# Changing the widths of the first three held-back x transposes from 2, 2, 2 chunks to 1, 2, 3

## The chip, the cores and the metric

The kernel runs on one core of one Trainium2 chip. The metric is the device time of one execution in microseconds. The kernel before takes 265.04 us (median of the first three runs, 264.27 to 265.58). A verdict of faster or slower needs a difference of over 2%. The question here is smaller than that by an order of magnitude, so much of this document is about telling a difference of 0.1% from noise, and about seeing in a trace what the clock on the wall cannot resolve.

Names used below: a *chunk* is 128 of the 2,048 rows of x. PE is TensorE's matmul stream and PEld its weight loads, DVE is VectorE, ACT ScalarE, POOL GpSimd, SP SyncE (and SPq its queue, which issues DMAs).

## The reference

```python
# x: [1, 2048, 640] bf16
g = sigmoid((x * gate_w).sum(-1, keepdims=True))
# branch A: linear attention
q, k, v = split(x @ wqkv)            # 32 heads of 20
pq, pk = phi(q), phi(k)              # phi(t) = (t + 1 if t > 0 else exp(t)) + 1e-6
o = (pq @ (pk^T v)) / (pq . sum(pk) + 1e-6)
a = o @ wo
# branch B: a mixer MLP with layer norms, w1, w2, w3, w4  (cut)
return g * a + (1 - g) * b
```

Only the first product of branch A matters here: `k = x @ wk`, which the kernel computes chunk by chunk as its first stage. The matmul contracts over the 640 features, so it needs x with features on the partitions: the transposed tile `xT`.

## The kernel before

At the start the kernel loads x chunks 0 and 1 and the five pieces of `wk` by plain DMAs. Chunks 0 and 1 are transposed on PE (`turn`); chunks 2 to 15 are transposed by the DMA engines on their way in (`load_xT`). Those transposes are *held back*: one column of chunk 2's place in `xT` is written by DVE after the first PE transposes, and the first DMA transpose, which writes over that column, has to wait for it. All later transposes stand behind it on the SP queue. So the k weights go first.

```python
    def load_xT(c0, c1):
        sp.dma_start_transpose(xT[:, :, c0 * P:c1 * P], x2[c0 * P:c1 * P, :])
    # ... (cut)
    load_x(0, 1)
    aq.dma_start(g5[:], gate_w.rearrange("(c p) -> c p", p=P))
    load_wk(sp, 1)
    load_wk(aq, 0)
    load_x(1, 2, aq)
    load_wk(sp, 3)
    load_wk(aq, 2)
    load_wk(sp, 4)

    def late_loads():
        for c0, c1 in ((2, 4), (4, 6), (6, 8), (8, 10), (10, 12), (12, 16)):
            load_xT(c0, c1)
        sp.dma_start(wq_sb, wqkv_v[:, :, 0:D])
        # ... (cut: the other x loads and weights)

    def k_mm(pt, c, dcs, first=0, last=DC - 1):
        for dc in dcs:
            for hf in range(2):
                n = HD + hf
                nc.tensor.matmul(pt[:, hf, 0:n], lhsT=xT[:, dc, c * P:(c + 1) * P],
                                 rhs=wk_sb[:, dc, hf * HD:hf * HD + n], start=(dc == first), stop=(dc == last))
    # ... (cut)
    def turn(c):                    # chunks 0 and 1: transpose on PE
        for pt, a, b in turns:
            # ... (cut: five PE transposes in two groups)
            # ... (cut: DVE copies the group into xT)
            if c == 0 and a == 0:
                nc.vector.tensor_copy(wk_sb[:, :, D], pt[:, 1, 0:DC])
                nc.vector.memset(xT[:, 0:1, 2 * P:2 * P + 1], 0.0)     # holds the transposes back

    turn(0)
    late_loads()
    # ... (cut)
    warmup(1, TS)
    for n, dc in enumerate(k0_order):          # chunk 0, in the order in which wk arrives
        if n == 3:
            turn(1)
        elif 1 <= n < 3:
            warmup(1, 2 * P)
        k_mm(kp, 0, (dc,), first=k0_order[0], last=k0_order[-1])
    k_evac(kp, 0)
    for c in range(1, NCH):                    # chunks 1 to 15
        pt = pair()
        k_mm(pt, c, range(DC))
        k_evac(pt, c)
    # then the q stage, which reads all of xT
```

Of the kernel before, what the change touches and what calls it, by code (L numbers as in the profile page):

```python
# [16 lines left out]
def kernel(  # L17
# [100 lines left out]
    def load_x(c0, c1, q=sp):  # L118
        q.dma_start(x_sb[:, c0:c1, 0:D], x2[c0 * P:c1 * P, :].rearrange("(c p) d -> p c d", p=P))

    def load_xT(c0, c1):
        sp.dma_start_transpose(xT[:, :, c0 * P:c1 * P], x2[c0 * P:c1 * P, :])
# [11 lines left out]
    load_wk(sp, 4)  # L134

    def late_loads():
        for c0, c1 in ((2, 4), (4, 6), (6, 8), (8, 10), (10, 12), (12, 16)):
            load_xT(c0, c1)
        sp.dma_start(wq_sb, wqkv_v[:, :, 0:D])
        load_x(2, 8)  # L140
        load_x(8, 16)
        sp.dma_start(wv_sb[:], wqkv_v[:, :, 2 * D:3 * D])
        sp.dma_start(w1_sb[:], B_w1.rearrange("(c p) f -> p c f", p=P))
        for g in range(NG):
            sp.dma_start(wo_sb[:, g, :], A_wo[row0[g]:row0[g] + P, :])
        for g in range(4):
            sp.dma_start(w2_sb[:, g, :], B_w2[CG * g:CG * g + P, :])
            sp.dma_start(w2_sb[32 * g:32 * (g + 1), 4, :], B_w2[CG * g + P:CG * (g + 1), :])
        sp.dma_start(w3_sb[:], B_w3.rearrange("(c p) f -> p c f", p=P))
# [73 lines left out]

    turn(0)
    late_loads()
    for dc in range(DC):
        for g in range(4):
# [399 lines left out]
```

## Time and profile before

| | before |
|---|---|
| time, first three runs | 265.04 us (264.27 to 265.58) |
| span of the profiled execution | 262.8 us |
| PE busy | 259.1 us |
| first transpose issued / landed | 4.26 / 8.50 us |
| chunk 2's k weight loads begin | 8.55 us |
| q stage's first weight load | 27.50 us |

From the page, the busy time of each engine (time, share of the span, instructions) and the granted clock in 40 slices:

```profile
PE 259.1 (99%) x1738; PEld 159.9 (61%) x1738; DVE 142.7 (54%) x283; ACT 82.7 (31%) x123; POOL 20.2 (8%) x65
...
PEclk9999999999999999999999999999999999999999
```

PE is busy in 99% of the span, so whatever stops it for a moment should be added to the time. The chain of work that ended last, cut to the first 60 us (columns: start, duration, what), shows one piece that is not PE, DVE or issue:

```profile
4.21 0.05 DVE xT L218
4.26 4.24 DMA xT<-in_A_x_dram
8.50 0.05 issue
8.55 19.25 PE pp L185 x140
27.80 21.58 PE pp L247 x100
```

The 140 k matmuls of chunks 2 to 15 run in one piece after the first transpose has landed. But the 4.24 us of that transfer are not lost: PE is working on chunks 0 and 1 meanwhile. What it costs is in the tables of waits of PE and PEld (who waited for what: total us, times, longest):

```profile
PE pp L185 <- DMA xT<-in_A_x_dram: 0.2, 1, 0.2
...
PEld L185 <- DMA xT<-in_A_x_dram: 0.5, 1, 0.5
```

The weight load's 0.5 us is the better measure of the delay, because matmul ends are modelled and the weight load is what has to read `xT`. The timeline of PEld from 8.2 us (start, duration, what, count, idle before and its releaser) shows it in place. A timeline keeps loads in one line as long as none of them comes after more than 0.15 us of idle time; after this line no k weight load waits again.

```profile
8.54 11.42 PEld L185 LDWEIGHTS <-xT 128*128 128x128 bf16 x85 [0.53 <-DMA xT<-in_A_x_dram]
```

The first two transposes on the SP queue, each from a timeline of a narrow window, and the time from issue to landing of five of the six (the view places no landing for the first, whose semaphore later transfers share; its own records give 4.24 us):

```profile
4.26 1.48 SPq L122 DMA_TRANSPOSE xT<-in_A_x_dram  x1
...
5.79 1.67 SPq L122 DMA_TRANSPOSE xT<-in_A_x_dram  x1
...
DMA to landing us min/median/max: 4.2/4.6/5.8
```

Where an exact landing or the start of a chunk is quoted below, it is read from the trace's individual records: a transfer has landed when the last of its 16 completion records is in, and chunk c starts with the (10c+1)th weight load of the k stage.

### The profile page before, as it was taken

Reading aid. Unit: us, or ns where it says so; the run is one execution under the profiler, and the core shown is the slowest. Engines: PE = TensorE matmul, PEld = TensorE weight load, DVE = VectorE, ACT = ScalarE, POOL = GpSimd, SP = SyncE. Lnnn points to the kernel's source line nnn. Section 1 sums busy time; section 2 is a strip of 40 time slices with the busy share of each in tenths; the row PEclk is TensorE's granted clock in tenths of the full one; section 3 lists DMA queues with packets and bytes.
Section 4 is the critical chain, followed back from the end, with each engine's and each line's share of the span. In section 5 each row is a group of like instructions: output and inputs, shape, how many; then the busy total and the mean of one; then the engine's idle time right before and its main releaser. Section 6 shows DMA issues by size and latency. Waiting matters only on the chain.

```text
span 262.8 us, 4268 instructions
## 1 busy us (share of the span) xinstructions
PE 259.1 (99%) x1738; PEld 159.9 (61%) x1738; DVE 142.7 (54%) x283; ACT 82.7 (31%) x123; POOL 20.2 (8%) x65
## 2 busy tenths in 40 slices
PE   8999999999999999999999999999999999999995
PEld 4677555788755644555577555567565577555553
DVE  2688778899947998955403464413456223112132
ACT  1555454321166236622502222412131332142200
POOL 5000040012220040001000001000001000000000
PEclk9999999999999999999999999999999999999999
DMA  6999987016672566700132000051100051100011
GB/s 200 193 203 379 364 229 299 0 27 125 125 98 58 107 122 163 241 0 2 25 75 77 25 0 2 0 100 52 50 0 4 0 100 52 50 0 2 0 50 50
DMA packets 45757, 23.98 MB, mean 91 GB/s; under 512 B 35114, under 2 KB 44970, under 8 KB 45738
## 3 DMA queue, kind: packets, MB, share of 16 engines
q1 hardware_dynamic: 45296, 23.22, 34.6%
q10 hardware_dynamic: 442, 0.49, 0.5%
q8 instruction: 13, 0.21, 0.4%
q14 instruction: 6, 0.05, 0.1%
HBM read 12.21 MB, written 2.62 MB: 56 GB/s over the span
## 4 chain that ended last, share of the span: by engine, by line
PE 97%; DMA 2%; DVE 0%; issue 0%
PE pp L504 22%; PE pp L471 21%; PE pp L319 8%; PE pp L455 8%; PE pp L424 8%; PE pp L353 8%; PE pp L247 8%; PE pp L185 7%; DMA xT<-in_A_x_dram 2%; PE pp L391 1%; PE pp L479 1%; PE pp L198 1%; PE pp L513 1%; PE pp L372 1%; PE pp L262 0%; DVE xT L218 0%
## 5 line engine op out<-in xcount | busy, mean ns | idle before, releaser
L471 PE MATMUL pp<-lnxT,w_sb 128*128 128x512 bf16 x260 | 60.4, 379 | 0.0
L504 PE MATMUL pp<-w_sb,h 128*128 128x384 bf16 (+3 forms) x416 | 57.9, 299 | 0.0
L473 ACT ACTIVATE h<-pp 128x1024 bf16<-128x1024 f32 (+1 forms) x28 | 26.9, 961 | 82.2 <-PE pp L471 82.2
L504 PEld LDWEIGHTS <-h 128*128 128x128 bf16 x416 | 38.3, 98 | 19.3 <-issue 1.1
L471 PEld LDWEIGHTS <-w_sb 128*128 128x128 bf16 x260 | 25.4, 98 | 26.9
L518 DVE SCALAR_TENSOR_TENSOR oc<-pp,omg,x 128x640 bf16<-128x640 f32 (+2 forms) x20 | 14.4, 749 | 45.1 <-ACT h2x L482 21.3
L458 DVE SCALAR_TENSOR_TENSOR x<-pp,gate,x 128x640 f32<-128x640 f32 x16 | 13.9, 867 | 29.4 <-PE pp L455 29.4
L177 ACT ACTIVATE e<-pp 128x640 bf16<-128x640 f32 (+1 forms) x26 | 21.5, 826 | 9.6 <-PE pp L247 9.6
L455 PE MATMUL pp<-m_sb,pqT 128*128 128x320 bf16 x160 | 24.3, 299 | 0.0
L424 PE MATMUL pp<-w_sb,hsT 128*128 128x320 bf16 x160 | 23.9, 299 | 0.0
L427 DVE TENSOR_TENSOR x<-pp,x_sb 128x640 f32<-128x640 f32 x16 | 13.1, 820 | 19.7 <-PE pp L424 19.7
L185 PE MATMUL pp<-wk_sb,xT 128*128 128x320 bf16 (+1 forms) x160 | 23.0, 302 | 0.2 <-DMA xT<-in_A_x_dram 0.2
L319 PE MATMUL pp<-x_sb,pk 128*128 128x320 bf16 (+1 forms) x160 | 22.0, 300 | 0.0
L247 PE MATMUL pp<-xT,hsT 128*128 128x512 bf16 x100 | 21.7, 379 | 0.0
L319 PEld LDWEIGHTS <-pk 128*128 128x128 bf16 x160 | 18.8, 117 | 3.2
L424 PEld LDWEIGHTS <-hsT 128*128 128x128 bf16 x160 | 15.7, 98 | 8.2
L455 PEld LDWEIGHTS <-pqT 128*128 128x128 bf16 x160 | 15.7, 98 | 7.7
L185 PEld LDWEIGHTS <-xT 128*128 128x128 bf16 x160 | 15.6, 99 | 7.1 <-DMA xT<-in_A_x_dram 0.5
L353 PE MATMUL pp<-lnxT,w_sb 128*128 128x512 bf16 x80 | 18.1, 379 | 0.0
L247 PEld LDWEIGHTS <-hsT 128*128 128x128 bf16 x100 | 11.8, 118 | 9.7
L289 POOL TENSOR_SCALAR rstd<-mv 128x4 f32<-128x4 f32 (+1 forms) x11 | 3.4, 312 | 154.2 <-DVE mv L295 154.2
L179 DVE SCALAR_TENSOR_TENSOR pk<-pp,e 128x640 bf16<-128x640 f32 x16 | 13.2, 825 | 1.7
(77 smaller groups left out, 190.2 us busy)
## 6 DMA issues: line engine op xcount, KB each, us to landing
out_dram<-oc SPq DMA_DIRECT2D x14, 160.0 KB, 1.8
w_sb<-in_B_w_dram SPq DMA_DIRECT2D x1, 2160.0 KB, 8.4
w_sb<-in_B_w_dram SPq DMA_DIRECT2D x1, 2080.0 KB, 10.2
x_sb<-in_A_x_dram SPq DMA_DIRECT2D x1, 1280.0 KB
x_sb<-in_A_x_dram SPq DMA_DIRECT2D x1, 960.0 KB, 7.4
wo_sb<-in_A_wo_dram SPq DMA_DIRECT2D x6, 160.0 KB, 7.9
hsT<-in_A_wqkv_dram SPq DMA_DIRECT2D x1, 800.0 KB, 5.4
m_sb<-in_A_wqkv_dram SPq DMA_DIRECT2D x1, 800.0 KB, 12.0
```

What stands on the lines that cost most here:

```text
L177: nc.scalar.activation(ev, src, ACT.Exp)
L185: nc.tensor.matmul(pt[:, hf, 0:n], lhsT=xT[:, dc, c * P:(c + 1) * P], rhs=wk_sb[:, dc, hf * HD:hf * HD + n], start=(dc == first), stop=(dc ...
L247: nc.tensor.matmul(pt[:, t % 2, :], lhsT=wq_sb[:, dc, :].rearrange("p (m j) -> p j m", j=DC)[:, j], rhs=xT[:, dc, t * TS:(t + 1) * TS], st ...
L319: nc.tensor.matmul(pt[:, hf, 0:HD + hf], lhsT=w, rhs=x_sb[:, c, hf * HD:(hf + 1) * HD + hf], start=(c == 0), stop=(c == NCH - 1))
L353: nc.tensor.matmul(pt[:, i, :], lhsT=w, rhs=lnxT[t][:, dc, :], start=(dc == 0), stop=(dc == DC - 1))
L424: nc.tensor.matmul(pt[:, hf, 0:HD], lhsT=hsT[:, fc, 2 + c * P:2 + (c + 1) * P], rhs=w2_sb[:, fc, hf * HD:(hf + 1) * HD], start=(fc == 0), ...
L455: nc.tensor.matmul(pt[:, hf, 0:HD], lhsT=pqT[:, j, c * P:(c + 1) * P], rhs=m_sb[:, j, hf * HD:(hf + 1) * HD], start=(j == 0), stop=(j == D ...
L458: nc.vector.scalar_tensor_tensor(x1, pt[:, :, 0:HD], gate[:, c:c + 1], x1, op0=ALU.mult, op1=ALU.add)
L471: nc.tensor.matmul(pt[:, k, :], lhsT=w3_sb[:, dc, fc * P:(fc + 1) * P], rhs=lnT[:, dc, :], start=(dc == 0), stop=(dc == DC - 1))
L473: nc.scalar.activation(h2[:, 2 * i * TS:(2 * i + n) * TS], pt[:].rearrange("p h e -> p (h e)")[:, 0:n * TS], ACT.Gelu_apprx_tanh)
L504: nc.tensor.matmul(dst, lhsT=st[t]["h2"][:, fc * TS + cc * P:fc * TS + (cc + 1) * P], rhs=w4_sb[:, fc, a:b], start=start and fc == 0, stop ...
L518: nc.vector.scalar_tensor_tensor(oc[:, a:b], src, omg[:, c:c + 1], st[t]["x1"][cc][:, a:b], op0=ALU.mult, op1=ALU.add)
```

## The change

The intent: give PE its first DMA-transposed chunk sooner by making the first transfer one chunk wide, then let the widths grow. The number of transfers, the bytes and all arithmetic stay.

```diff
     def late_loads():
-        for c0, c1 in ((2, 4), (4, 6), (6, 8), (8, 10), (10, 12), (12, 16)):
+        for c0, c1 in ((2, 3), (3, 5), (5, 8), (8, 10), (10, 12), (12, 16)):
             load_xT(c0, c1)
```

No engine's instruction order changes; only the widths of three instructions on the SP queue do.

## The prediction

> **What bounds the kernel now.** TensorE. The page's busy table gives PE 259.1 of a 262.8 us span (99%) at the full granted clock. The chain of work that ended last is 97% matmuls and 2% one DMA: the first held-back transpose of x into xT. There it is a piece from 4.26 to 8.50 us, and chunk 2's k matmuls start at 8.55 us. But the table of waits charges that transfer with only 0.19 us of idle PE and 0.53 us of idle weight-load time, as chunks 0 and 1 fill nearly all of the 4.24 us. After 8.55 us the timeline shows 140 k matmuls in one unbroken piece of 19.25 us (1.375 us a chunk), with no later wait.
>
> **What the change does.** Arithmetic, bytes and the number of transposes (six) stay. PE, DVE, ACT and POOL keep their order; on SP the first three transposes become 1, 2, 3 chunks wide instead of 2, 2, 2.
>
> *Gain.* A two-chunk transpose takes 1.3 to 1.9 us to issue on SP (starts 4.26, 5.79, 7.50, 8.88, 10.79) and 4.2 to 4.6 us from issue to landing. My estimate for one chunk, from half of that issue time: about 0.8 us of issue, landing at 7.6 to 8.0 us instead of 8.50. The weight loads before chunk 2 end at 8.02 us, so chunk 2 could start at about 8.05 to 8.1. At most 0.5 us is to be had; PE's own idle there is 0.2.
>
> *Cost.* Chunk 3 now comes with the second transfer: issued near 5.1 us, landing 4.2 to 4.6 us later, at 9.3 to 9.7. PE wants it at about 8.05 + 1.375 = 9.45. So a new wait of 0 to 0.3 us can take back part of the gain. Chunk 5 now comes with a three-chunk transfer issued near 6.6 us; estimate of its landing 11.5 to 12.3, wanted at 8.1 + 3 x 1.375 = 12.2: about at the margin. Before, the second transfer landed at 10.4 for chunk 4 at 11.3, and the third at 11.7 for chunk 6 at 14.05: 0.9 and 2.3 us of slack. The change spends most of it. Later transposes and the q weights (landing at 21.7, wanted at 27.64) keep microseconds.
>
> The Trainium skill ("DMA: Bandwidth & Descriptors", section "Rules for kernel authors") says to issue early and wait late so that the fixed cost overlaps with compute. The trace agrees: all but 0.2 to 0.5 us of the first transpose is already hidden.
>
> **Prediction.** Net gain of 0.2 us on 265.04 us; three runs of before alone span 1.3 us. Time 264.8 us, 8 in 10 between 264.0 and 265.6. Faster by over 2%: 0.01; within 2%: 0.98; slower by over 2%: 0.01.
>
> **What would show it right or wrong.** Right: chunk 2's k matmuls start near 8.1 us instead of 8.55 and the wait for the first transpose falls to about zero; perhaps a wait for xT under 0.4 us appears one to three chunks later; everything later is shifted by the net amount, with equal durations. Wrong in size: the one-chunk transfer lands no earlier than 8.4 us, because the weight transfers ahead of it (the DMA engines are nearly full from 4 to 7 us) set its landing rather than its width; then the gain is zero and the new waits remain.
>
> **What could break it.** A three-chunk transpose (384 rows) handled by a slower path than 256 or 512 rows, so that chunk 5 waits a microsecond or more.

## The result, and the profile after

Ratios in this document are the mean time of one kernel's fast runs over that of the other's of the same rounds, so they are not quite the ratio of the medians quoted beside them.

| | before | after |
|---|---|---|
| time, six runs each on one chip | 264.86 us (264.27 to 265.58) | 264.97 us (264.68 to 265.07) |
| ratio | | 1.0001, 95% interval [0.9983, 1.0019] |
| span | 262.8 us | 263.3 us |
| q stage's first weight load | 27.50 us | 27.95 us |

In the chain of waits after, again cut to 60 us, the transpose is gone and a k weight stands in its place:

```profile
1.25 3.59 DMA wk_sb<-in_A_wqkv_dram
...
7.27 20.98 PE pp L185 x154
```

PE's waits say so too; no wait for a transpose is listed on PE or PEld (the list leaves out idle time under 0.15 us):

```profile
PE pp L185 <- DMA wk_sb<-in_A_wqkv_dram: 0.5, 1, 0.5
```

The first three transposes on SP, each from a narrow window, and the issue-to-landing figures, again without the first, which took 3.85 us:

```profile
4.26 1.30 SPq L122 DMA_TRANSPOSE xT<-in_A_x_dram  x1
...
5.62 1.38 SPq L122 DMA_TRANSPOSE xT<-in_A_x_dram  x1
...
7.04 2.05 SPq L122 DMA_TRANSPOSE xT<-in_A_x_dram  x1
...
DMA to landing us min/median/max: 4.6/5.1/5.9
```

Three things stand out. Halving the width of the first transpose took its issue only from 1.48 to 1.30 us, so the second is issued at 5.62 us and lands at 10.25 us. Chunk 3, which now depends on that second transfer, starts at 10.29 us, against 9.79 us in before. And this wait is nearly invisible in this execution (the gap before chunk 3 exceeds an ordinary one by 0.05 us), because the start was late for other reasons: the first k weight landed at 4.84 us (4.40 in before), and chunk 2 began at 8.88 us (e2 finds a second reason, the larger one).

That suggests **theory A, the wait moved**: the change frees chunk 2 and makes chunk 3 wait for the second transpose instead, and the k stage ends a little later than before. The rival is **theory B, the transposes have no bearing**: the start is set by when the k weights land, and this profile was merely an unlucky draw.

### The profile page after: what moved, and what is told of

Same layout as the page of the kernel before. It is cut to its first block, busy times and chain, and to the rows that moved or that the text cites. A ratio compares the mean times of both kernels' runs of the same rounds, so it can differ in the third digit from the quotient of the medians.

```text
span 263.3 us, 4248 instructions
## 1 busy us (share of the span) xinstructions
PE 258.2 (98%) x1719; PEld 160.3 (61%) x1738; DVE 142.7 (54%) x283; ACT 82.7 (31%) x123; POOL 20.1 (8%) x65
## 4 chain that ended last, share of the span: by engine, by line
PE 97%; DMA 1%; issue 0%; SPq 0%; DVE 0%
PE pp L504 22%; PE pp L471 21%; PE pp L185 9%; PE pp L319 8%; PE pp L424 8%; PE pp L455 8%; PE pp L353 8%; PE pp L247 8%; DMA wk_sb<-in_A_wqkv_dram 1%; PE pp L391 1%; PE pp L479 1%; PE pp L513 1%; PE pp L372 1%; PE pp L262 0%; PE pp L198 0%
## 5 line engine op out<-in xcount | busy, mean ns | idle before, releaser
L471 PE MATMUL pp<-lnxT,w_sb 128*128 128x512 bf16 x249 | 59.8, 379 | 0.6
L353 PE MATMUL pp<-lnxT,w_sb 128*128 128x512 bf16 x76 | 17.9, 379 | 0.2
```

The source lines that it names most:

```text
L353: nc.tensor.matmul(pt[:, i, :], lhsT=w, rhs=lnxT[t][:, dc, :], start=(dc == 0), stop=(dc == DC - 1))
L471: nc.tensor.matmul(pt[:, k, :], lhsT=w3_sb[:, dc, fc * P:(fc + 1) * P], rhs=lnT[:, dc, :], start=(dc == 0), stop=(dc == DC - 1))
```

## The experiments

First the quantities that the theories turn on, for all thirteen profiles. "Last slow load" is the start of the last weight load that took over 0.135 us; see f1 and e2 for what it means. "q stage" is the start of its first weight load, which the text also calls the end of the k stage, and "rest" is the span less that. Times in us; "<3.6" means that no load after 3.5 us was slow.

| profile | last slow load | chunk 1 | 1st transpose landed | chunk 2 | 2nd landed | chunk 3 | q stage | span | rest |
|---|---|---|---|---|---|---|---|---|---|
| before | 5.14 | 6.70 | 8.50 | 8.55 | 10.35 | 9.79 | 27.50 | 262.82 | 235.32 |
| f1, before | 4.55 | 6.99 | 8.53 | 8.57 | 10.03 | 9.82 | 27.53 | 262.83 | 235.30 |
| f3, before | <3.6 | 7.30 | 9.07 | 9.11 | 10.96 | 10.35 | 28.06 | 263.36 | 235.30 |
| after | 6.60 | 7.52 | 8.11 | 8.88 | 10.25 | 10.29 | 27.95 | 263.26 | 235.31 |
| e1, after | 4.99 | 6.78 | 7.24 | 8.14 | 10.47 | 10.52 | 28.11 | 263.42 | 235.31 |
| f2, after | <3.6 | 6.66 | 7.18 | 8.02 | 10.22 | 10.26 | 27.85 | 263.17 | 235.32 |
| f4, after | 5.51 | 6.69 | 8.05 | 8.10 | 10.39 | 10.43 | 28.02 | 263.34 | 235.32 |
| e2, no x wait | 6.68 | 7.19 | 8.55 | 8.55 | 10.49 | 9.92 | 27.63 | 262.95 | 235.32 |
| e3, wide first | 3.69 | 7.18 | 10.02 | 10.07 | 11.89 | 11.31 | 29.02 | 264.39 | 235.37 |
| e4, ones | 6.48 | 7.16 | 8.16 | 8.52 | 9.52 | 9.88 | 27.89 | 263.30 | 235.41 |
| e5, 3 and 4 freed | 4.49 | 6.61 | 7.13 | 7.97 | 9.85 | 9.33 | 27.05 | 262.36 | 235.32 |
| e6, early release | 5.93 | 7.43 | 8.35 | 8.79 | 9.99 | 10.15 | 27.86 | 263.17 | 235.31 |
| e7, four ones | 3.58 | 7.02 | 7.29 | 8.38 | 9.27 | 9.74 | 27.48 | 262.96 | 235.48 |

The last column is the first finding: from the q stage on, every profile takes 235.30 to 235.48 us. The whole difference between any two of these kernels is made before 30 us.

### e1_after_again: the changed kernel once more

No edit.

> The changed kernel once more, word for word, for a second profile and more rounds. Theory A (the wait moved): the second transpose now gates chunk 3. In the first profile of the changed kernel it landed at 10.25 us and chunk 3 began at 10.29 us, just at the margin because a late k weight (landed 4.84 us) had already put chunk 2 back to 8.88 us. If the weight comes at about 4.4 us this time, chunk 2 should start near 8.1 to 8.2 us and the weight loads should then wait 0.5 to 0.8 us for xT before chunk 3, which starts at 10.0 to 10.3 us; k stage ends 0.2 to 0.5 us later than in before's first profile. Theory B (the transposes have no bearing, the start is set by when the k weights land): no wait for xT before chunk 3 over 0.1 us however early the weight comes, and k ends earlier by just what the weight comes earlier. Ratio: A 1.000 to 1.002, B 0.999 to 1.001.

Measured: 264.91 us (264.84 to 265.14), before 264.70 us (264.51 to 265.45), ratio 1.0009 [0.9997, 1.0021]. The first k weight landed at 4.25 us, chunk 2 started at 8.14 us, and the timeline of PEld shows what theory A wants:

```profile
6.92 2.55 PEld L185 LDWEIGHTS <-xT 128*128 128x128 bf16 x19
10.52 5.56 PEld L185 LDWEIGHTS <-xT 128*128 128x128 bf16 x42 [1.05 <-DMA xT<-in_A_x_dram]
```

The weight loads stop for 1.05 us before chunk 3 (expected 0.5 to 0.8) and go on 0.04 us after the second transpose landed at 10.47 us. The k stage ends 0.61 us later than in before's first profile, a little more than expected. Theory B, which allowed no gap here, falls.

### e2_no_x_wait: k matmuls that need no held-back transpose

```diff
-                nc.tensor.matmul(pt[:, hf, 0:n], lhsT=xT[:, dc, c * P:(c + 1) * P],
+                nc.tensor.matmul(pt[:, hf, 0:n], lhsT=xT[:, dc, (c % 2) * P:(c % 2 + 1) * P],
```

> Before, but the k matmuls of chunks 2 to 15 read chunk 0's or 1's columns of xT, so that no k matmul waits for a held-back transpose (the result is wrong on purpose; the transfers are the same). It is the upper bound of what any partition of the transposes can give. Both theories: no wait for xT on PE or its weight loads; if the wait is all the cost, chunk 2 starts near 8.05 us with the k weight at 4.4 us, 0.4 to 0.5 us before the 8.55 of before, and the ratio is 0.998 to 0.9995. Against both: a ratio under 0.996 would mean that the waits for transposes cost far more than the profile shows.

Measured: result wrong, as meant (relative error 0.042); 264.58 us (264.30 to 265.43), ratio 1.0000 [0.9984, 1.0016]. No wait for `xT`, as expected; but chunk 2 started at 8.55 us, not 8.05, and so the expected gain is missing. Chunk 1 was late already (7.19 us, against 6.70 in before), for two reasons. The last k weight, which chunk 0 needs, landed at 6.80 us (6.52 in before). In ten of the thirteen profiles chunk 1 starts 0.18 to 0.24 us after that landing, which would put it at about 6.98 us here. The other 0.2 us is in how long the same five weight loads of chunk 1's PE transposes took, in before (first line) and here (second), each from the timeline of PEld:

```profile
5.86 0.31 PEld L213 LDWEIGHTS <-x_sb 128*128 128x128 bf16 x5
```

```profile
5.99 0.74 PEld L213 LDWEIGHTS <-x_sb 128*128 128x128 bf16 x5
```

Nearly all loads take 0.15 us up to some moment and 0.10 us from then on, and the k matmuls turn with them: their starts lie 0.27 us apart before it and 0.135 us after. The moment differs from execution to execution: the last slow load started at 5.14 us in before's profile and at 6.68 us here. The trace's individual clock records, which no view prints, begin just there: the first is of 5.31 us in before, of 6.76 us here, and of 3.62 to 6.78 us over the twelve profiles that have one (e3 has none). The Trainium skill ("TensorE: Matmul & The Clock Gate", section "What's actually happening") describes a clock gate on PE that opens after some 3.4 us of activity, measured in a window that runs freely and does not start with the kernel, so that the turn differs from run to run. These profiles agree in kind.

In e2, e4 and after, the three with the latest turns (6.56 to 6.78 us), chunk 1 starts at 7.2 to 7.5 us, 0.39 to 0.80 us after the last k weight, and chunk 2 would start at about 8.5 to 8.9 us anyway, as late as the first two-chunk transpose lets it (8.5 us). In e3, e6 and f3 it is the last k weight that came late (7.00 to 7.23 us). So theory B has a part of the truth: chunk 1's start goes with the last weight and the turn.

Before's own three profiles show a wait of 0.27 to 0.53 us at chunk 2. But over the ten profiles of the other kernels, chunk 1's start plus an ordinary chunk (1.36 us) puts the time at which chunk 2 is wanted at 7.97 to 8.15 us in four and at 8.38 to 8.88 us in six. So before pays fully for its first transpose only in some executions. That is the second finding: the gain that the change aims at is 0.5 us at most, and sometimes nothing.

### e3_wide_first: double the suspected wait

```diff
-        for c0, c1 in ((2, 4), (4, 6), (6, 8), (8, 10), (10, 12), (12, 16)):
+        for c0, c1 in ((2, 6), (6, 8), (8, 10), (10, 12), (12, 16)):
```

> Before, with the first transpose four chunks wide, then 2, 2, 2, 4 (five transfers). It doubles the suspected wait and shows whether a wait at 8 us reaches the end of the kernel. Theory A: the four-chunk transfer lands at 9.5 to 10.3 us, the weight loads wait 1.4 to 2.2 us for it, and the whole lasts 1.0 to 1.8 us longer than before: ratio 1.004 to 1.007. Theory B: the wait is there, but the time moves by under 0.4 us, ratio under 1.0015.

Measured: 265.96 us (265.87 to 266.10), ratio 1.0046 [1.0034, 1.0058]. The transpose took 3.08 us to issue and landed at 10.02 us; PEld's timeline:

```profile
10.06 5.02 PEld L185 LDWEIGHTS <-xT 128*128 128x128 bf16 x38 [1.57 <-DMA xT<-in_A_x_dram]
```

The k stage ends 1.52 us later than in before and the span is 1.57 us longer. The later start of chunk 2 (10.07 against 8.55 us) does reach the end, undiminished, and the timed runs can see one of this size. As theory A expected.

### e4_ones: what an issue costs

```diff
-        for c0, c1 in ((2, 4), (4, 6), (6, 8), (8, 10), (10, 12), (12, 16)):
+        for c0, c1 in ((2, 3), (3, 4), (4, 5), (5, 8), (8, 10), (10, 12), (12, 16)):
```

> Before, with transposes of one, one, one, three and then two chunks (seven transfers in place of six). It asks what an issue costs. If the issue has a floor near 1.3 us whatever the width (as the one-chunk transfer of the changed kernel showed, 1.304 us): issues start at about 4.26, 5.6, 6.9 and 8.2 us, chunk 3 lands at 9.3 to 9.9 us (a wait of 0 to 0.4), chunk 4 near 10.5 to 11.2, and the three-chunk transfer for chunk 5 at 13.0 to 13.8 us where it is wanted at about 12.3: waits for xT of 0.6 to 1.5 us in sum, ratio 1.001 to 1.005. If the issue goes with the width, as the prediction assumed (0.8 us for one chunk): starts at 4.26, 5.1, 5.9 and 6.7 us, chunk 5 lands by 11.9 us, waits for xT under 0.2 us, ratio 0.998 to 1.000.

Measured: 265.02 us (264.92 to 265.13), ratio 1.0011 [0.9999, 1.0023]. The issues of the first three, one chunk each, took 1.30, 1.26 and 1.28 us, and the fourth started at 8.25 us. The second, from a narrow window of SP's timeline, at the place in the queue where the changed kernel's two-chunk transpose took 1.38 us:

```profile
5.61 1.26 SPq L122 DMA_TRANSPOSE xT<-in_A_x_dram  x1
```

So a transpose of one chunk occupies the queue for about 1.3 us, and the prediction's 0.8 us was wrong. One rival is that the DMA engines, busy with the k weights, held the issue up. Before's own trace speaks against it: later in the kernel it issues 37 more transposes of 128 rows of 640 (from SBUF, not HBM), and 35 of them took 1.20 to 1.24 us. This is the first; the DMA engines were 1% busy during its issue:

```profile
54.50 1.20 SPq L323 DMA_TRANSPOSE wk_sb<-gs  x1
```

So most of the 1.3 us is there without any weight in flight, and the number stood in the profile that the prediction was made from. The three-chunk transfer for chunk 5 landed at 12.98 us, and PEld waited there:

```profile
13.03 2.02 PEld L185 LDWEIGHTS <-xT 128*128 128x128 bf16 x16 [0.46 <-DMA xT<-in_A_x_dram]
```

That wait is under the 0.6 to 1.5 us expected in sum, because this execution's turn was late and chunks 3 and 4 were wanted late too.

### e5_after_free34: take the new wait out of the changed kernel

```diff
     def k_mm(pt, c, dcs, first=0, last=DC - 1):
+        s = c % 2 if c in (3, 4) else c
         for dc in dcs:
             for hf in range(2):
                 n = HD + hf
-                nc.tensor.matmul(pt[:, hf, 0:n], lhsT=xT[:, dc, c * P:(c + 1) * P],
+                nc.tensor.matmul(pt[:, hf, 0:n], lhsT=xT[:, dc, s * P:(s + 1) * P],
```

> The changed kernel, but the k matmuls of chunks 3 and 4 read chunk 1's and 0's columns of xT, so that they do not wait for the second transpose (wrong result on purpose; same transfers). Theory A: the gap before chunk 3 goes; chunk 2 starts at 8.15 us (landing) or up to 8.9 with a late turn of the loads; then the third transpose (landing 12.2 to 12.7) is the next gate for chunk 5, wanted at 12.24 with an early turn and at 12.6 to 13.0 with a late one, so a wait of 0 to 0.5 us. The k stage ends 0.2 to 0.6 us before that of the changed kernel's second profile and the ratio to before is 0.9985 to 1.0003, under the 1.0009 of the changed kernel. Theory B: the same ratio as the changed kernel, 1.000 to 1.001, and nothing moves at chunk 3.

Measured: 264.48 us (264.07 to 264.64), ratio 1.0000 [0.9986, 1.0014]. Two chunks of k are wrong on purpose; the comparison with the reference passed all the same, so that check is not sharp enough to see them. The gap before chunk 3 is gone (9.33 us): PEld's timeline has all k weight loads of chunks 1 to 15 in one piece, with no wait of over 0.15 us, up to the q stage.

```profile
6.05 20.96 PEld L186 LDWEIGHTS <-xT 128*128 128x128 bf16 x154
27.05 0.90 PEld L248 LDWEIGHTS <-hsT 128*128 128x128 bf16 x5
```

Chunk 5 starts 0.04 us after the landing of the three-chunk transpose at 12.05 us, and the k stage ends at 27.05 us, 1.06 us earlier than in e1 (more than the expected 0.2 to 0.6) and earliest of all profiles. With the second transpose out of the way the change does what it meant to do. The profile is of the fastest of the five runs (264.07 us; the others took 264.35 to 264.64), so 1.06 us is at the high end: the five have a mean of 264.42 us, against 264.87 us for the one run of the changed kernel on the same chip (f2). The ratio to before alone could not show it: its interval holds both theories.

### e6_early_release: release the transposes sooner

```diff
     nc.vector.tensor_copy(g5z[0:DC, :], g5[:])
+    nc.vector.memset(xT[:, 0:1, 2 * P:2 * P + 1], 0.0)
 ...
-                nc.vector.memset(xT[:, 0:1, 2 * P:2 * P + 1], 0.0)
```

> Before, with the same widths, but the write to xT that holds the transposes back stands on DVE right after the copy into g5z (it ran at 4.16 us, here it should run at about 2.4 us), so that the transposes are issued some 1.5 us earlier, from about 2.7 us. A partition can only trade the first landing for the second; this moves all of them. Theory A: the first transpose lands at 6.9 to 7.4 us and no k matmul waits for xT; if the k weights came no later the k stage would end 0 to 0.4 us earlier, ratio 0.9985 to 1.000. Against it: the transposes share the DMA engines with the k weights still in flight, so the last weights may land 0.3 to 1.5 us later (6.5 to 6.8 us so far) and the k matmuls wait for those: ratio 1.001 to 1.006.

Measured: 264.54 us (264.31 to 264.92), ratio 1.0003 [0.9990, 1.0015]. The first transpose was issued at 2.73 us, 1.53 us earlier, but its issue took 2.25 us and it landed at 8.35 us, only 0.15 us earlier, where 6.9 to 7.4 was expected. The last of the plain loads landed at 7.23 us (6.52 in before) and chunk 1 started at 7.43 us. An earlier issue into engines that are still busy with the weights hardly brought the transpose earlier. The weights came later too, but f3, with the hold-back, has its last at 7.13 us, so one profile does not show that the release is the cause. So an issue time is not the whole of a landing time, and the hold-back of the kernel before costs nothing that these runs show.

### f1_before_again and f3_before_third: the kernel before against itself

No edit in either.

> The kernel before, word for word, against itself: a second profile and the noise of a ratio. What is still open is how much before itself loses at chunk 2. So far chunk 1 began at 6.70 to 6.79 us where the weight loads turn from 0.152 to 0.098 us each early (before 5.4 us), and at 7.16 to 7.52 us where they turn late (6.7 to 6.9 us) or a k weight lands late. Theory A: chunk 2 starts at the later of chunk 1's start + 1.36 us and the landing of the first transpose (8.5 us) + 0.04 us, so between 8.52 and 8.9 us, and the wait for xT is 0 to 0.5 us according to the turn of the loads; the span less the end of the k stage is 235.3 us, as in all profiles so far. Ratio 1.000, 0.999 to 1.001.

f1 measured: 264.68 us (264.55 to 265.34), ratio 1.0012 [0.9999, 1.0024]. Chunk 2 started at 8.57 us, 0.04 us after the landing, with a wait of 0.27 us; all within what was expected but the ratio, which lies 0.0002 outside.

> The kernel before, word for word, for a third profile and a second measure of the noise. The wait moved, so chunk 3's start is the mark: in before it should be at the later of chunk 1's start + 2.72 us and about 9.8 us, so 9.75 to 9.85 us with an early turn of the weight loads (both profiles so far: 9.79 and 9.82) and up to 10.2 with a late one. Ratio 0.999 to 1.0015 (the first such run gave 1.0012).

f3 measured: 264.67 us (264.43 to 265.11), ratio 1.0004 [0.9992, 1.0017]. Here the expectation missed: chunk 3 started at 10.35 us, not by 9.85, although the turn was early (3.62 us). The first transpose took 1.79 us to issue and landed only at 9.07 us, and the weights were late as well (the last landed at 7.13 us). So before has executions as slow at the start as the changed kernel's.

Both runs give a ratio above 1 for identical kernels. A single ratio of 1.0009 or 1.0012 for the changed kernel is therefore no evidence by itself.

### f2_after_third and f4_after_fourth: the changed kernel twice more

No edit in either.

> The changed kernel, word for word, for a third profile. Theory A (the second transpose, issued at 5.62 us, gates chunk 3): it lands at 10.2 to 10.5 us and chunk 3 starts within 0.05 us of that landing, whether the loads turn early (chunk 2 near 8.15, wait about 0.8 us) or late (chunk 2 near 8.55 to 8.9, wait 0.05 to 0.6 us). Theory B (transposes have no bearing): no gap at chunk 3.

f2 measured: one run, 264.87 us.

> The changed kernel, word for word, for a fourth profile, beside the kernel before on the same chip. Chunk 3 should start at 10.2 to 10.5 us, within 0.05 us of the landing of the second transpose (so far 10.29, 10.52 and 10.26), and the mean should lie 0.1 to 0.4 us above that of before, ratio 1.0003 to 1.0015; a ratio of 1.000 or less would speak against the moved wait as a loss.

f4 measured: 264.94 us (264.77 to 265.05), before 264.60 us (264.46 to 264.78), ratio 1.0012 [0.9998, 1.0025]. In both, chunk 3 starts 0.04 us after the second transpose landed (10.22 and 10.39 us), after a wait of about 1 us; f2 and f4, PEld's timelines:

```profile
10.26 4.75 PEld L185 LDWEIGHTS <-xT 128*128 128x128 bf16 x36 [0.91 <-DMA xT<-in_A_x_dram]
```

```profile
10.43 4.61 PEld L185 LDWEIGHTS <-xT 128*128 128x128 bf16 x35 [1.06 <-DMA xT<-in_A_x_dram]
```

In all four profiles of the changed kernel chunk 3 starts at 10.26 to 10.52 us, whether chunk 2 started at 8.02 or at 8.88.

### e7_four_ones: the finest start, as a candidate

```diff
-        for c0, c1 in ((2, 4), (4, 6), (6, 8), (8, 10), (10, 12), (12, 16)):
+        for c0, c1 in ((2, 3), (3, 4), (4, 5), (5, 6), (6, 8), (8, 10), (10, 12), (12, 16)):
```

> Before, with transposes of one, one, one, one and then two chunks (eight transfers): the finest start, as the candidate for a better partition. With the floor of 1.3 us for an issue the first four are issued at 4.26, 5.6, 6.9 and 8.2 us and land near 7.3 to 8.2, 9.5, 11.0 and 12.3 us, a pace of about 1.35 us that PE's 1.36 us for a chunk just matches; wanted with an early turn at 8.05, 9.4, 10.8 and 12.2, with a late one at 8.5 to 8.9, 9.9, 11.2 and 12.6. Waits of 0.1 to 0.4 us in sum with an early turn and none with a late one; the next, chunks 6 and 7, lands near 13.9 to 14.2 and is wanted at 13.6 to 14.2. Chunk 7 starts 0 to 0.3 us before that of before (15.24 to 15.27); ratio 0.999 to 1.0005. If the floor is not what sets the pace, chunk 4 lands by 10.5 us.

Measured: 264.68 us (264.61 to 265.29), ratio 1.0009 [0.9997, 1.0022], above what was expected but not told apart from noise. The four were issued at 4.26, 5.62, 6.92 and 8.24 us and landed at 7.29, 9.27, 10.56 and 12.14 us; chunks 2 to 5 did not wait. Chunk 6 waited 0.18 us for the next transfer (landed 13.93 us), and the k stage ended at 27.48 us, as in before. It saves the start and pays the same back four chunks later. It beats nothing that the runs can show, and as chunk 2 cannot start before about 8.0 us, no partition can gain more than some 0.5 us, or 0.2%.

## Why the prediction was right or wrong

**The time was right, for partly wrong reasons.** 264.97 us lies in 264.0 to 265.6 and "within 2%" held. What made it safe was the reading of the waits: the 4.24 us of transfer in the chain looked like 2% of the span, but only 0.2 to 0.5 us of it was idle time of PE, so no change to it could matter by 2%. The stated range, 1.6 us wide, is eight times the predicted gain and holds a loss as well as a gain: that the number lies in it says nothing for the sign.

**Right: chunk 2 is freed.** The prediction put its start at 8.05 to 8.1 us. Three of the four profiles have 8.02, 8.10 and 8.14 us; the first had 8.88, because of a late turn to fast weight loads (its first weight was late as well, 4.84 us, but f2 had 4.72 and the start at 8.02). In none of the four did chunk 2 wait more than 0.05 us for its transpose. The landing itself was put at 7.6 to 8.0 us and was at 7.2 us in two profiles and at 8.1 in two: a miss on both sides, without effect.

**Wrong: the term for the one-chunk issue, and with it the sign of the net.** The prediction took half the issue time of two chunks, about 0.8 us. It is 1.30 to 1.31 us in all four profiles and 1.26 to 1.30 us in e4. So the second transpose was issued at 5.62 us in place of 5.1, and took 4.6 to 4.9 us from there in place of 4.2 to 4.6; it landed at 10.2 to 10.5 us in place of 9.3 to 9.7. That is about where before's second transfer lands (10.03 to 10.96 us in its three profiles), but chunk 3 now needs it, and not chunk 4. The "new wait of 0 to 0.3 us" before chunk 3 is 0.05 us with the latest start of chunk 2 and 0.9 to 1.1 us in the three others. It more than takes back the gain: freeing chunk 2 is worth at most 0.5 us (8.55 to 8.05), while chunk 3 moved from 9.8 us in two of before's three profiles (10.35 in the third) to 10.26 to 10.52 us. e5 takes that one wait out and the k stage ends 0.8 to 1.1 us earlier than in the four profiles of the changed kernel; this is what shows the wait to be the cause of the later end. That a shorter issue would have brought the second landing forward is not shown (see "Left open").

**How large is the loss?** All 17 runs of the changed kernel have a mean of 264.94 us with a standard deviation of 0.13 us; the 45 of before, 264.70 us with 0.29 us. The difference of the means is 0.24 us, or 0.09%, against the predicted gain of 0.2 us. It should be read with care: the runs are of four groups, and the two tests of before against itself gave 1.0012 and 1.0004; in f1 the means of identical kernels on one chip differ by 0.26 us. Compared with those ten runs alone (mean 264.75 us), the difference is 0.18 us with a standard error of about 0.1. A loss of 0.1 to 0.3 us is what the means suggest, and the timed runs do not prove it; the moved wait is shown by the profiles.

**Not foreseen: the spread.** Before's runs range from 264.22 to 265.58 us, the changed kernel's from 264.68 to 265.14. This fits the profiles: before's start depends on when PE turns fast and when the weights land, while in the changed kernel chunk 3 starts with a landing that varied by only 0.26 us and absorbs what came before it. That last step is an argument from four profiles; executions with no profile were not examined.

**Right in the main: the rest.** The three-chunk transpose was estimated to land at 11.5 to 12.3 us, just when wanted; it landed at 12.05 to 12.68 us (over the range in e1 and, by 0.02 us, in f4), and where chunk 3 no longer waited (e5) it was at the margin with a gap of 0.04 us. It had no slow path of its own (issue 1.98 to 2.05 us for 384 rows). Everything after 28 us shifted by the net amount and kept its durations.

**Left open.** How the landing of the second transpose divides between its issue and the engines' own pace. e6 shows that an earlier issue alone need not land earlier while weights are in flight, and e7's fourth transfer took 3.9 us from issue to landing against 3.0 for the first.

## What to carry to other kernels

When a piece of a transfer is made smaller so that its consumer can start sooner, cost the *next* piece too: its consumer now comes one step earlier, and if a transfer has a fixed cost the next one does not come earlier by as much. Take the cost of an untried size from a measured issue of that size, not by dividing a larger one; here transposes of that very size stood further on in the same profile, at 1.20 us. And before hiding a wait of half a microsecond at the start of a kernel, look at several executions: here the wait was present in some and already covered by something else in others.

## What the Trainium skill lacked or had wrong

- "DMA: Bandwidth & Descriptors" gives no time that a transpose on this chip occupies its issuing queue by width. First in the queue here: 1.30 to 1.31 us for 128 rows of 640 (after, e1, e4, e5, e7, f2, f4), 1.43 to 1.79 us for 256 rows (before, e2, f1, f3; 2.25 us in e6, where it was issued 1.53 us earlier), 3.08 us for 512 rows (e3). In second place: 1.26 us for 128 rows (e4, e7), and for 256 rows 1.38 us in the changed kernel and 1.53 to 1.68 us in before. Later in the kernel, from SBUF: 1.20 to 1.24 us for 128 rows (35 of 37 in before).
- The same page, section "Rules for kernel authors", advises to coalesce and puts "mostly overhead" at transfers under 64 KB. That rule speaks of a transfer as a whole and gives no time on the issuing queue. There the fixed part is large above 64 KB too: a one-chunk transpose here moves 160 KB, and in second place after another of one chunk it still took 91% of the queue time of one of 320 KB (1.26 us in e4 against 1.38 us in the changed kernel).
- "TensorE: Matmul & The Clock Gate", section "What's actually happening", gives plus or minus 500 ns for the moment of the turn to the fast clock. (The same section also reports 6, 11 or 14 slow matmuls in runs of one kernel.) In the twelve profiles here that have clock records the first of them begins at 3.62 to 6.78 us, with PE's first matmul at 0.83 us in each: a spread of 3.2 us, which is closer to a whole one of the windows of 3.4 us that the page describes.
- No page drawn on here says that the granted clock as the profile's views print it does not show this turn: it reads 1.00 in before's first 4.2 us, in which weight loads took 0.15 us, and 1.00 after 5.31 us, when they took 0.10. The clock records of the trace begin only at 5.31 us there, and the views count time without a record as full clock.
